# Dilated/sliding attention ahead of a squared-ReLU FFN: attention steps placed by tables, dilated values spread early, loads merged and reordered

## Chip, cores, metric

One core of one Trainium2 chip. The metric is the device time of one execution in microseconds (us); each kernel was run several times, on several chips. Of the kernel before, the record marks some as slow, being over 1.5% above its fastest. Its medians include them, the ratios leave them out.

## The reference

Attention over 8 batches, 8 heads, 576 positions, 64 values a head. Heads 0 to 3 see the last 32 positions, heads 4 to 7 see every fourth of the last 128. The result, 4608 tokens of 512 values, goes through an FFN with 2048 hidden values.

```python
def _attn_ref(q, k, v):
    scores = scale * np.matmul(q, k.transpose(0, 1, 3, 2))
    rel = pos[:, None] - pos[None, :]
    mask_plain = (rel >= 0) & (rel < 32)
    mask_dil = (rel >= 0) & (rel < 128) & (rel % 4 == 0)
    # ... where(mask, scores, -1e9), softmax over the last axis ...
    return np.matmul(attn, v)

def _moe_ref(x, w_in, w_out):
    h = np.maximum(x @ w_in, 0.0)
    return h * h @ w_out
```

## The kernel before

Heads are handled in four pairs, 0 and 1 plain, 2 and 3 dilated, in the order 0, 2, 1, 3. For each pair and batch there are seven kinds of step: transpose q, transpose k (TensorE, then copies out of PSUM by the scalar engine for plain q and by the vector engine for the rest), scores in two halves (matmuls, Exp on the scalar engine, mask multiply on the vector engine), for dilated pairs the spread of the values (two vector copies from the place where they were loaded, tile `vd`, into the block-diagonal tile `vbd`), and PV in two halves (value and sum matmuls into PSUM, Ln and Exp on the scalar engine for the reciprocal, a vector multiply into `xT`).

The FFN runs in nine tiles of 512 tokens, 32 groups of four 128x512 matmuls each: 16 of the first layer (relu on the scalar engine, square on the vector engine) and 16 of the second. A group's place is called a slot. Attention steps of batch b are emitted between the groups of tile b-1, and each engine's timeline shows its instructions in the order of emission. PV is the product of probabilities and values; PSUM is the memory in which matmul results stand until an engine copies them out.

```python
p_pool  = ...(name="p", bufs=2)                     # masked probabilities
ps_f    = ...(name="ps_f", bufs=4, PSUM)            # FFN, batch 0's scores, spare PV
ps_a    = ...(name="ps_a", bufs=2, PSUM)            # transposes, scores
ps_o, ps_d = ... bufs=1 each, PSUM                  # PV values, PV sums

def spread_v(b, e):                                 # dilated pairs only
    for hl in range(2):
        rows = slice(64 * hl, 64 * hl + 64)
        nc.vector.tensor_copy(vbd[b % 2][rows, e, 0:8, rows], vds[b][rows, e - NE // 2, :, :]...)

def attention_steps(b, base, pace, at):
    steps = []
    for x, e in enumerate(ORDER):                   # ORDER = (0, 2, 1, 3)
        s = base + pace * x
        if e >= NE // 2:
            steps.append((s + at[4], lambda e=e: spread_v(b, e)))
        steps.append((s + at[0], lambda e=e: t_main(b, e, "q")))
        steps.append((s + at[1], lambda e=e: t_main(b, e, "k")))
        steps.append((s + at[2], lambda e=e: scores(b, e, 0)))
        steps.append((s + at[3], lambda e=e: scores(b, e, 1)))
        steps.append((s + at[4], lambda e=e: pv(b, e, 0)))
        steps.append((s + at[5], lambda e=e: pv(b, e, 1)))
    return [(min(s, 2 * NF * b - 1), f) for s, f in steps]

for e in ORDER:                                     # all loads go out by GpSimd
    load_qk(0, [e])
    load_v(0, [e])
# ... w_in in two pieces, w_out in four ...
zero_halves(vbd[1], nc.gpsimd)                      # two memsets
for e in ORDER:
    load_qk(1, [e])
    load_v(1, [e])

first_attention(0)                                  # batch 0, a fixed three-stage loop
# ...
steps += attention_steps(1, 13, 6, (0, 1, 3, 4, 6, 8))
steps += attention_steps(2, G, 7, (0, 1, 4, 5, 7, 9))       # G = 32 slots
for b in range(3, B):
    steps += attention_steps(b, G * (b - 1) - 6, 8, (0, 2, 5, 6, 9, 12))
# ... emit group g, then all steps whose slot is <= g ...
```

The softmax here doesn't subtract the row's maximum and nothing guards it: scores larger than these inputs give would overflow.

## Time and profile before

| | before |
|---|---|
| median of 3 runs (all 7 of the first study rounds, 4 of them marked slow) | 384.47 us (383.85, from 378.11 to 386.62) |
| span of the profiled run | 376.8 us |
| TensorE busy | 318.7 us, 85% |
| vector, scalar, GpSimd busy | 200.4, 214.8, 90.7 us |

The page of the profiled run of the kernel before, engines (PE is TensorE's matmuls, PEld its weight loads, DVE the vector engine, ACT the scalar engine, POOL GpSimd) and four rows of its 40 slices (a digit is the busy share of a slice of 9.4 us in tenths; PEclk is TensorE's granted clock):

```profile
PE 318.7 (85%) x2389; PEld 177.7 (47%) x2432; DVE 200.4 (53%) x568; ACT 214.8 (57%) x437; POOL 90.7 (24%) x132
...
PE   1657979558789969996999699969998899999995
...
DVE  7784436445746756475647564765457552411410
...
PEclk9999989959999999999999999998999699999999
DMA  9999998294008900980098009900110002002002
```

TensorE stays at nine tenths only in the last fifth, where no attention is left. From slice 14 on it dips once in every fourth slice, which is once in each FFN tile, and deeper in slices 8 and 9, the end of tile 0. The clock row dips in some of the same places. Loads are dense in the first six slices and come in bursts after that.

### The profile page before, as it was taken

What the parts mean: (1) busy time and instruction counts of PE and PEld (TensorE: products, weight loads), DVE (VectorE), ACT (ScalarE), POOL (GpSimd) and SP (SyncE); (2) the same over time, 40 slices, a digit from 0 to 9 for tenths busy, and PEclk for the clock granted to TensorE, in tenths of its full rate; (3) what the DMA queues carried; (4) which work ended last, traced back from release to release, by engine and by line L of the source; (5) the groups of instructions that cost most, each with busy time, mean ns of one, the idle gap of its engine ahead of it and who ended that gap; (6) DMA issues with size and microseconds to landing.
All of it is one profiled execution on the core that took longest, in us unless ns stands there. A gap on an engine that the chain in (4) does not pass through costs nothing.

```text
span 376.8 us, 6323 instructions
## 1 busy us (share of the span) xinstructions
PE 318.7 (85%) x2389; PEld 177.7 (47%) x2432; DVE 200.4 (53%) x568; ACT 214.8 (57%) x437; POOL 90.7 (24%) x132
## 2 busy tenths in 40 slices
PE   1657979558789969996999699969998899999995
PEld 1534534334445535554555355535554455544542
DVE  7784436445746756475647564765457552411410
ACT  3545744537656775577656765675578444633621
POOL 8952862261007300620062007200000000000000
PEclk9999989959999999999999999998999699999999
DMA  9999998294008900980098009900110002002002
GB/s 104 150 214 208 158 139 113 57 146 42 1 30 131 143 3 7 181 114 2 4 177 121 1 3 168 133 0 2 57 56 3 0 30 84 0 30 84 0 30 84
DMA packets 51917, 28.32 MB, mean 75 GB/s; under 512 B 27696, under 2 KB 45744, under 8 KB 51888
## 3 DMA queue, kind: packets, MB, share of 16 engines
q0 software_dynamic: 46560, 18.38, 43.0%
q1 hardware_dynamic: 5184, 9.44, 6.8%
q8 instruction: 19, 0.31, 0.3%
q10 hardware_dynamic: 144, 0.11, 0.1%
q14 instruction: 10, 0.08, 0.1%
HBM read 36.81 MB, written 9.44 MB: 123 GB/s over the span
## 4 chain that ended last, share of the span: by engine, by line
PE 67%; ACT 13%; DVE 11%; issue 5%; POOL 2%; DMA 1%; ACTq 0%; DVEq 0%; POOLq 0%
PE pf L336 30%; PE pf L347 26%; ACT qT L193 5%; DVE kbd L198 4%; PE po L279 3%; PE pa L170 3%; ACT h2T L340 3%; PE pd L279 2%; DVE vbd L154 2%; ACT rec L282 2%; PE pa L230 2%; ACT rec L281 2%; DMA qb<-in_q_dram 1%; DVE xT L285 1%; DVE h2T L341 1%
## 5 line engine op out<-in xcount | busy, mean ns | idle before, releaser
L336 PE MATMUL pf<-xT,w_in_sb 128*128 128x512 bf16 x555 | 140.3, 390 | 1.9 <-DVE xT L285 0.5
L347 PE MATMUL pf<-w_out_sb,h2T 128*128 128x512 bf16 x554 | 135.9, 382 | 1.2
L340 ACT ACTIVATE h2T<-pf 128x512 bf16<-128x512 f32 x144 | 85.3, 595 | 36.3 <-PE pf L336 34.7
L341 DVE TENSOR_TENSOR h2T<-h2T 128x512 bf16<-128x512 bf16 x144 | 60.1, 424 | 69.7 <-ACT h2T L340 68.7
L336 PEld LDWEIGHTS <-w_in_sb 128*128 128x128 bf16 x576 | 60.5, 115 | 48.3 <-issue 6.0
L347 PEld LDWEIGHTS <-h2T 128*128 128x128 bf16 x576 | 51.5, 98 | 49.9 <-issue 1.1
L281 ACT ACTIVATE rec<-pd 128x288 f32<-128x288 f32 (+2 forms) x60 | 24.7, 411 | 41.5 <-PE pd L279 41.5
L353 ACT COPY osb<-pf 128x512 f32<-128x512 f32 x36 | 21.1, 585 | 42.3 <-PE pf L347 42.0
L279 PE MATMUL po<-pt,vbd 128*128 128x96 bf16 (+1 forms) x300 | 21.9, 207 | 26.0 <-DVE vbd L154 22.1
L279 PEld LDWEIGHTS <-vbd 128*128 128x128 bf16 x320 | 20.6, 104 | 41.1 <-DVE vbd L154 26.1
L236 ACT ACTIVATE pt<-pa 128x352 bf16<-128x352 f32 (+2 forms) x56 | 28.0, 501 | 18.1 <-PE pa L230 8.7
L193 ACT COPY qT<-pa 64x288 bf16<-64x288 bf16 x64 | 30.3, 474 | 11.7 <-PE pa L170 11.2
L285 DVE TENSOR_TENSOR xT<-po,rec 128x288 bf16<-128x288 f32 x30 | 13.7, 458 | 40.6 <-ACT rec L282 39.5
L116 POOL DMA_DIRECT2D qb<-in_q_dram x10 | 7.5, 746 | 104.7 <-PE pa L170 80.3
L198 DVE COPY kbd<-pa 64x288 bf16<-64x288 bf16 x64 | 30.4, 475 | 0.7
L282 ACT ACTIVATE rec<-rec 128x320 f32<-128x320 f32 (+1 forms) x64 | 28.4, 443 | 2.0
L138 POOL DMA_DIRECT2D vd<-in_v_dram x32 | 19.4, 609 | 30.0 <-DMA qb<-in_q_dram 14.4
L134 POOL DMA_DIRECT2D vbd<-in_v_dram x32 | 24.1, 762 | 4.1 <-DMA w_in_sb<-in_moe_w_in_dram 4.0
L292 DVE TENSOR_TENSOR xT<-po,rec 128x320 bf16<-128x320 f32 (+1 forms) x30 | 13.8, 460 | 20.1 <-ACT rec L282 17.1
L180 DVE COPY qT<-pa 64x288 bf16<-64x288 bf16 x64 | 19.4, 304 | 7.5 <-PE pa L170 6.8
L170 PE MATMUL pa<-mk,qb 72*128 72x72 bf16 x256 | 14.8, 205 | 8.6 <-DMA qb<-in_q_dram 8.6
L279 PE MATMUL pd<-pt,mk 128*128 128x160 bf16 (+5 forms) x150 | 21.3, 243 | 0.0
(48 smaller groups left out, 240.3 us busy)
## 6 DMA issues: line engine op xcount, KB each, us to landing
out_dram<-osb SPq DMA_DIRECT2D x36, 256.0 KB, 2.0
qb<-in_q_dram POOLq DMA_DIRECT2D x12, 288.0 KB, 6.7
kb<-in_k_dram POOLq DMA_DIRECT2D x12, 288.0 KB, 8.4
vbd<-in_v_dram POOLq DMA_DIRECT2D x32, 72.0 KB, 8.7
vd<-in_v_dram POOLq DMA_DIRECT2D x32, 64.0 KB, 4.9
w_in_sb<-in_moe_w_in_dram POOLq DMA_DIRECT2D x2, 1024.0 KB, 11.0
w_out_sb<-in_moe_w_out_dram POOLq DMA_DIRECT2D x4, 512.0 KB, 17.5
qb<-in_q_dram POOLq DMA_DIRECT2D x8, 144.0 KB, 4.9
```

The costliest lines, as they stand in the source:

```text
L134: nc.gpsimd.dma_start(dst[rows, e, :, rows], v[b, h].rearrange("(i p) d -> p i d", p=64))
L170: nc.tensor.transpose(pv_[:, hl, PT * pos : PT * pos + PT], rbs[b][nm][:, 2 * e + hl, P * jp : P * jp + P], ident[0:PT, 0:PT])
L193: nc.scalar.copy(qT[rows, e, :].rearrange("p (u a j) -> p j u a", a=JT // 2, j=2)[:, jj, :, :], src.rearrange("p (a u) -> p u a", a=JT // 2),)
L198: nc.vector.tensor_copy(kbd[rows, e, :, rows].rearrange("p i (u a j) -> p j i u a", a=JT // 2, j=2)[:, jj, :, :, :], src.rearrange("p (a i ...
L236: nc.scalar.activation(pt[:, off : off + n], ps[:, 0:n], ACT.Exp, scale=SCALE)
L279: nc.tensor.matmul(oo, lh, rh, start=(x == 0), stop=(x == len(g) - 1), skip_group_check=True)
L281: nc.scalar.activation(rec[:, 0:n], d[:, 0:n], ACT.Ln)
L282: nc.scalar.activation(rec[:, 0:n], rec[:, 0:n], ACT.Exp, scale=-1.0)
L336: nc.tensor.matmul(ps1[:, :], w_in_sb[:, kt, 512 * (f // 4) + f % 4 : 512 * (f // 4) + 512 : 4], xT[:, kt, tk0 : tk0 + NT], start=(kt == 0 ...
L340: nc.scalar.activation(h2[:, f, :], ps1[:, :], ACT.Relu)
L341: nc.vector.tensor_tensor(out=h2[:, f, :], in0=h2[:, f, :], in1=h2[:, f, :], op=ALU.mult)
L347: nc.tensor.matmul(cur[m][:, :], h2[:, f, P * m : P * m + P], w_out_sb[:, f, :], start=(f == 0), stop=(f == NF - 1),)
```

## The change

The intent: place every step of the first three batches by a table, so that no chain of waits is left bare at a tile's end; make the steady pipeline of batches 3 to 7 one slot longer between k and scores (q and k go out a slot earlier; with the base at -7 instead of -6, scores and PV keep their slots); emit the dilated spread with the q transposes instead of with PV; and bring q and k ahead of the values in larger transfers.

```diff
-    p_pool = ...(tc.tile_pool(name="p", bufs=2))
+    p_pool = ...(tc.tile_pool(name="p", bufs=4))
+FIRST = "q0 k0 q2 a0 b0 k2 k1 a2 q1 q3 v2 o0 a1 b1 k3 o1 v3 b2 p0 a3 b3 o2 p2 p1 o3 p3".split()
+EARLY = {
+    1: ("15:q0 16:k0 18:q1 19:k1 22:q2 22:a0 23:b0 24:k2 24:v2 24:a1 25:o0 26:v3 26:b1 27:q3 27:p0 27:a2 "
+        "27:o1 29:k3 29:b2 29:p1 29:o2 30:a3 30:b3 30:p2 31:o3 31:p3"),
+    2: ("0:k0 0:q0 5:a0 5:k2 6:v2 9:q2 9:v3 9:b0 12:o0 13:a2 13:b2 15:p0 15:k1 15:q1 18:k3 18:o2 18:a1 21:q3 "
+        "21:p2 23:o1 24:b1 24:a3 25:b3 25:p1 28:o3 31:p3"),
+}
-    for e in ORDER:
-        load_qk(0, [e])
-        load_v(0, [e])
+    load_qk(0, [0])
+    load_qk(0, [2, 3])
+    load_qk(0, [1])
+    load_v(0, [0, 2, 1, 3])
     ... w_in in pieces of 512, 512 and 1024 columns instead of two of 1024 ...
     zero_halves(vbd[1], nc.gpsimd)
-    for e in ORDER:
-        load_qk(1, [e])
-        load_v(1, [e])
+    load_qk(1, [0, 1, 2, 3])
+    load_v(1, [0, 1, 2, 3])
+    ... in step(): pv(b, e, "op".index(what), spare=early and what == "p")    # early is b < 2; before, batch 0 only ...
-    first_attention(0)
+    for code in FIRST:
+        step(0, code)
-    steps += attention_steps(1, 13, 6, (0, 1, 3, 4, 6, 8))
-    steps += attention_steps(2, G, 7, (0, 1, 4, 5, 7, 9))
+    ... batches 1 and 2 from EARLY: "slot:step" ...
     for b in range(3, B):
-        steps += attention_steps(b, G * (b - 1) - 6, 8, (0, 2, 5, 6, 9, 12))
+        steps += attention_steps(b, G * (b - 1) - 7, 8, (0, 2, 6, 7, 10, 13, 0))   # last: the spread
```

In the codes q and k are transposes, a and b the score halves, v the spread, o and p the PV halves; the digit is the pair.

`spare` now holds for batch 1 too. Its second PV half writes to tiles of `ps_f` instead of waiting for the single `ps_o` and `ps_d` tiles.

More of the change, by code (lines that the diff above doesn't have):

```diff
@@ L13 @@
 RES = 4
+ORDER = (0, 2, 1, 3)
+FIRST = "q0 k0 q2 a0 b0 k2 k1 a2 q1 q3 v2 o0 a1 b1 k3 o1 v3 b2 p0 a3 b3 o2 p2 p1 o3 p3".split()
+EARLY = {
+    1: (
+        "15:q0 16:k0 18:q1 19:k1 22:q2 22:a0 23:b0 24:k2 24:v2 24:a1 25:o0 26:v3 26:b1 27:q3 27:p0 27:a2 "
+        "27:o1 29:k3 29:b2 29:p1 29:o2 30:a3 30:b3 30:p2 31:o3 31:p3"
+    ),
+    2: (
+        "0:k0 0:q0 5:a0 5:k2 6:v2 9:q2 9:v3 9:b0 12:o0 13:a2 13:b2 15:p0 15:k1 15:q1 18:k3 18:o2 18:a1 21:q3 "
+        "21:p2 23:o1 24:b1 24:a3 25:b3 25:p1 28:o3 31:p3"
+    ),
+}
 def _masks() -> np.ndarray:
@@ L72 @@
     vd_pool = ctx.enter_context(tc.tile_pool(name="vd", bufs=2))
-    p_pool = ctx.enter_context(tc.tile_pool(name="p", bufs=2))
+    p_pool = ctx.enter_context(tc.tile_pool(name="p", bufs=4))
     r_pool = ctx.enter_context(tc.tile_pool(name="r", bufs=2))
@@ L294, in pv, with step @@
             )
-    ORDER = (0, 2, 1, 3)
+    def step(b: int, code: str):
+        what, e = code[0], int(code[1])
+        first, early = b == 0, b < 2
+        if what in "qk":
+            t_main(b, e, what)
+        elif what in "ab":
+            scores(b, e, "ab".index(what), *((ps_f, "pf") if first else ()))
+        elif what == "v":
+            spread_v(b, e)
+        else:
+            pv(b, e, "op".index(what), spare=early and what == "p")
     def attention_steps(b: int, base: int, pace: int, at):
-        steps = []
+        out = []
         for x, e in enumerate(ORDER):
-            s = base + pace * x
-            if e >= NE // 2:
-                steps.append((s + at[4], lambda e=e: spread_v(b, e)))
-            steps.append((s + at[0], lambda e=e: t_main(b, e, "q")))
-            steps.append((s + at[1], lambda e=e: t_main(b, e, "k")))
-            steps.append((s + at[2], lambda e=e: scores(b, e, 0)))
-            steps.append((s + at[3], lambda e=e: scores(b, e, 1)))
-            steps.append((s + at[4], lambda e=e: pv(b, e, 0)))
-            steps.append((s + at[5], lambda e=e: pv(b, e, 1)))
-        return [(min(s, 2 * NF * b - 1), f) for s, f in steps]
-    def first_attention(b: int):
-        o = ORDER
-        for x in range(NE + 2):
-            if x >= 2 and o[x - 2] >= NE // 2:
-                spread_v(b, o[x - 2])
-            for nm, half in (("q", 0), ("k", 1)):
-                if x < NE:
-                    t_main(b, o[x], nm)
-                if 1 <= x <= NE:
-                    scores(b, o[x - 1], half, ps_f, "pf")
-                if x >= 2:
-                    pv(b, o[x - 2], half, spare=half == 1)
+            for what, off in zip("qkabopv", at):
+                if what != "v" or e >= NE // 2:
+                    out.append((base + pace * x + off, b, f"{what}{e}"))
+        return out
     def ffn_groups(t: int):
@@ L375 @@
     nc.vector.tensor_copy(mask_d[:, 352:416], mk[:, 96:160])
-    for e in ORDER:
-        load_qk(0, [e])
-        load_v(0, [e])
-    for c in range(2):
+    load_qk(0, [0])
+    load_qk(0, [2, 3])
+    load_qk(0, [1])
+    load_v(0, [0, 2, 1, 3])
+    for c0, c1 in ((0, 512), (512, 1024), (1024, 2048)):
         nc.gpsimd.dma_start(
-            w_in_sb[:, :, 1024 * c : 1024 * c + 1024],
-            moe_w_in[:, 1024 * c : 1024 * c + 1024].rearrange("(kt p) f -> p kt f", p=P),
+            w_in_sb[:, :, c0:c1], moe_w_in[:, c0:c1].rearrange("(kt p) f -> p kt f", p=P)
         )
@@ L400 @@
         groups += ffn_groups(t)
-    steps += attention_steps(1, 13, 6, (0, 1, 3, 4, 6, 8))
-    steps += attention_steps(2, G, 7, (0, 1, 4, 5, 7, 9))
+    for b, table in EARLY.items():
+        for x in table.split():
+            slot, code = x.split(":")
+            steps.append((G * (b - 1) + int(slot), b, code))
     for b in range(3, B):
-        steps += attention_steps(b, G * (b - 1) - 6, 8, (0, 2, 5, 6, 9, 12))
+        steps += attention_steps(b, G * (b - 1) - 7, 8, (0, 2, 6, 7, 10, 13, 0))
     steps.sort(key=lambda x: x[0])
@@ L407 @@
         t = g // G
-        if g % G == 0:
-            if t + 2 < B:
-                load_qk(t + 2, [0, 1, 2, 3])
-                load_v(t + 2, [0, 1, 2, 3])
+        if g % G == 0 and t + 2 < B:
+            load_qk(t + 2, [0, 1, 2, 3])
+            load_v(t + 2, [0, 1, 2, 3])
         group()
         while steps and steps[0][0] <= g:
-            steps.pop(0)[1]()
+            step(*steps.pop(0)[1:])
 _INS = ['q', 'k', 'v', 'moe_w_in', 'moe_w_out']
```

## The prediction

> **What bounds it.** I cut the run into stages first, by one table of engine time per stretch. Columns: stretch, its length, then busy time and (in brackets) instruction count of the matmul engine, weight loads, vector, scalar and GpSimd engine, then granted clock, DMA share, GB/s.
>
> ```profile
> 0.00:31.50 31.50, 13.64 (x159) 11.21 (x160) 23.34 (x58) 13.92 (x30) 24.12 (x35) 1.00 1.09 162
> 31.50:82.20 50.70, 38.83 (x286) 21.39 (x291) 24.31 (x69) 26.17 (x55) 25.71 (x37) 0.89 0.99 131
> 82.20:124.50 42.30, 36.68 (x302) 20.18 (x307) 25.29 (x73) 27.66 (x58) 9.62 (x14) 0.97 0.60 61
> 124.50:317.40 192.90, 174.42 (x1398) 98.18 (x1424) 113.36 (x336) 122.62 (x255) 31.27 (x46) 0.97 0.38 60
> 317.40:376.80 59.40, 55.11 (x252) 26.76 (x254) 14.07 (x33) 24.42 (x42) 0.00 (x0) 1.00 0.11 40
> ```
>
> They are: attention of batch 0 alone; FFN tile 0 with batch 1 beside it; tile 1 with batch 2; tiles 2 to 6 with batches 3 to 7; tiles 7 and 8 and the last store, with no attention left. TensorE is the bound from 31.5 us on, and its queue runs in program order, so its idle time is what can be won: 11.9 us in tile 0, 5.6 in tile 1, 18.5 in tiles 2 to 6 (3.7 a tile). The last stage is almost full (27.7 us a tile). Where a steady tile loses it, the matmul engine's timeline says; the brackets hold the idle time before a row and its releaser:
>
> ```profile
> 162.26 0.39 PE L230 MATMUL pa<-qT,kbd 128*128 128x96 bf16 x5 [0.49 <-DVE kbd L198]
> ...
> 174.01 1.03 PE L336 MATMUL pf<-xT,w_in_sb 128*128 128x512 bf16 x4
> 178.01 0.35 PE L279 MATMUL po<-pt,vbd 128*128 128x96 bf16 x5 [2.98 <-DVE vbd L154]
> ```
>
> The same two waits return in every steady tile (2.98 to 3.19 and 0.47 to 0.49). The copy waited for, the spread of the dilated values, is cheap; the vector engine was held up before it:
>
> ```profile
> 174.57 0.43 DVE L341 TENSOR_TENSOR h2T<-h2T 128x512 bf16<-128x512 bf16 x1 [0.44 <-ACT h2T L340]
> 177.01 0.42 DVE L341 TENSOR_TENSOR h2T<-h2T 128x512 bf16<-128x512 bf16 x1 [2.02 <-ACT h2T L340]
> 177.36 0.60 DVE L154 COPY vbd<-vd 64x512 bf16<-64x512 bf16 x2
> ```
>
> The square at 177.01 waits for a relu, and the scalar engine was copying the next q for 1.92 us from 174.44. Relu, square, spread and PV matmul stand in four queues behind that copy; the spread's data had been there for long.
>
> Tile 0 loses most at its end, where batch 1's last steps were all clamped to the last slot (a slot is one FFN group of four matmuls, 0.865 us) and run as a bare latency chain:
>
> ```profile
> 72.22 0.34 PE L279 MATMUL po<-pt,vbd 128*128 128x32 bf16 x5 [1.65 <-DVE xT L292]
> ...
> 77.09 0.26 PE L215 MATMUL pa<-qT,kbd 128*128 128x96 bf16 x1 [3.85 <-DVE kbd L184]
> ...
> 81.19 0.48 PE L279 MATMUL po<-pt,vbd 128*128 128x96 bf16 x5 [1.46 <-DVE xT L285]
> ```
>
> **The Trainium skill.** "TensorE: Matmul & The Clock Gate", Part 1, says that about a 3.4 us idle window drops the TensorE clock to half, until about as long a busy one. The trace agrees at gaps near that length: after the 3.19 us gap before 253.83, eight FFN matmuls took 3.28 us, where elsewhere eight take 1.89. Of five equal gaps only two were followed by this, as a free-running window would have it. The same page ("Architectural detail") calls the scalar and vector engines strict FIFO; the hold-up above is that. "SBUF — State Buffer", "Who interferes with whom", says a 2-port vector copy and a GpSimd instruction lock each other out for a whole instruction. It agrees: the spread's median is 291 ns, but one took 2074 ns beside the GpSimd memset of 17.9 to 22.0 us. "DMA: Bandwidth & Descriptors", "Bandwidth", favours larger transfers. Here a 144 KB q load lands in 4.9 us and a 288 KB one in 6.7, but in the first 30 us the queues share a rate of 104 to 214 GB/s that is already saturated, so I give merging little.
>
> **The change, part by part.** No arithmetic is added or removed; the compiled TensorE queue has 4866 rows before and after.
>
> *Steady tiles.* Spread moves from the slot of its PV step to ten slots earlier, with the q transposes. That removes the 2.98 us. Scores move from three slots after the k transposes to four (0.865 us more slack, against a wait of 0.49), which removes that too. A tile without both: 37.9 - 2.98 - 0.49 = 34.4. A check from below: 128 FFN matmuls at 0.216 are 27.7; attention adds, from start-to-start times, 8 transpose groups at 0.26, 8 PV halves at 0.36 and 1.5 for scores, together 6.5: 34.2. The extra scalar slack is real but not large: the scalar engine is busy 15.07 us in the first-layer half of a tile (20.2 us now, 17.2 then), 88%. I take 34.5. Five tiles: 172.5 against 192.9. Of the 20.4, some 3.5 are the two half-clock stretches after the gaps (these tiles' halves are 21.9 and 23.1 where the others are 20.2).
>
> *Tile 1.* Batch 2's table spreads its steps over slots 0 to 31 instead of bunching them. The early waits (1.29, 1.67, 1.40, 0.49 and the slow matmuls at 82 to 85.5) should mostly go; but two scores come three slots after their transposes behind a busy vector queue, and the last PV half is in slot 31, so the next tile waits for Ln, Exp and multiply (0.43 + 0.44 + 0.46, with latencies 1.5). 34.5 + 2.5 = 37.0 against 42.3.
>
> *Tile 0.* Batch 1 starts two slots later, in slot 15, and spreads its last PV steps over slots 25 to 31; k to score is now six slots, not two, for the first head pair (a 2.32 us wait). In the last five slots I count 7.7 us of TensorE work (5 groups at 0.865, 4 scores, 6 PV halves, 2 transpose groups) and 9.2 us of scalar work (4 exp at 0.5, seven Ln/Exp pairs at 0.87, two output copies). So it is scalar-bound there, and then the chain of the last half remains: 3 to 4 us of idle at the end, and 1 us of slow clock after it. 34.5 + 4 + 1 = 39.5 against 50.7. Loads do not stop it: the moved bytes up to slot 15 are as before and in the old run all weights were in by about 36 us, the q and k of batch 1 would follow by about 43 (estimate: 1.18 MB at the 176 GB/s of that stretch), and slot 15 comes at about 41 (28 + 15 x 0.865), slot 22 at 48.
>
> *Start.* q and k of all pairs now come ahead of the values, which are written in small pieces, and the steps interleave so that a wait of one pair is filled by another. The first two loads are in the same place, so the first transposes stay at 5.07 us. Then the vector queue bounds: two k copies of 1.93, two dilated q of 1.26, two dilated k of 1.76, eight masks 2.9, eight output multiplies 3.7, spreads 0.6 and 3.0 (the memset is still near), in sum 20.1 us from 6.8, plus 1 us waiting for q of pair 2: about 28 us, and 0.5 for the last chain. The old one finished its last multiply at 33.3. I take 4.5 us off: 31.5 becomes 27.0. The first third of w_in arrives in 512 columns, so weights do not take over: about 2.3 MB at 140 GB/s is 16 to 18 us.
>
> *Rest.* Tiles 7 and 8 are untouched: 59.4. Sum: 27.0 + 39.5 + 37.0 + 172.5 + 59.4 = 335.4, against 376.8. The measured time is 1.75 above the span (378.55), so 337.2. The unprofiled runs of before are slower than the profiled one (384.47 against 378.55); I read that as more of the five gaps falling into the slow clock, 1.7 us each, and fewer such gaps are left after. I add 1: 338.
>
> **The rivals.** *The wait moves to the scalar engine.* At 88% in the first-layer halves, relus may fall behind by more than the four PSUM buffers of the FFN. For it: the 1.92 us q copies. Against it: four buffers are 3.4 us of run-ahead, and the old stall came from the spread, not from an FFN matmul waiting. It would return 1 to 2 us a tile: 343 to 348. *Loads bound the first 70 us.* DMA is at about full share until 60 us; with FFN starting earlier and batch 1 in four large loads, a value load could land after slot 24, and the in-order vector queue would hang behind its spread. For it: the loads of batch 1 end near 49 us, the first spread of batch 1 comes at about 50. It would eat 3 to 6 us of tile 0: 341 to 344. *Only the spread counts*: the tables gain nothing on tiles 0 and 1 because scalar work is the same and bunched at their ends. Then 384.47 less 20 and 4.5, about 360; against it, the old chains from 70 to 82 us had both engines idle most of the time. *Better than thought*: start at 24, tile 0 at 37, tile 1 at 35 give 328 to 330.
>
> **Range and chances.** The steady saving alone is 5% and its cause is seen in each tile; losing it all and the rest as well is needed for no gain. The range is the sum of the rivals' sizes: 329 to 350. Faster by over 2% 0.97, within 2% 0.02, slower 0.01.
>
> **What would show it.** The spread should vanish as a releaser of PV matmuls from tile 2 on; steady tiles should take 34 to 35 us at clock 1.00; FFN should start at 26 to 29 us; tile 0 should end with one gap of 3 to 4 us, and its length be about 40. Wrong would be: FFN matmuls waiting for relu buffers, first transposes or spreads of batch 1 waiting for loads, or a steady tile above 36.

## The result

| | before | after |
|---|---|---|
| median | 384.67 us (4 runs) | 338.07 us (4 runs, 337.76 to 338.37) |
| ratio, 95% interval | | 0.8796 (0.8733 to 0.8859) |
| span of the profiled run | 376.8 us | 336.3 us |
| TensorE busy, idle | 318.7, 58.1 us | 309.4, 26.9 us |

A ratio is the mean time of one kernel's fast runs over that of the other's of the same rounds, so not quite the ratio of the medians quoted beside it. The page of the changed kernel, the same rows (a slice is 8.4 us here):

```profile
PE 309.4 (92%) x2432; PEld 175.7 (52%) x2432; DVE 200.4 (60%) x568; ACT 211.5 (63%) x437; POOL 87.3 (26%) x127
...
PE   1438999989999999999999999999999999999995
...
DVE  7797457969755784587549664966486724303400
...
PEclk9999999999999999999999999999999999999999
```

Vector work is the same 200.4 us to the digit. TensorE is at nine tenths from the fifth slice to the last but one, but for one eight, and the clock dips are gone. The same table by stages as in the prediction, the stages cut at the same events (first FFN matmul; start of tiles 1, 2 and 7):

```profile
0.00:31.00 31.00, 13.27 (x161) 11.03 (x161) 25.06 (x57) 12.93 (x29) 22.92 (x33) 1.00 1.06 150
31.00:67.20 36.20, 34.88 (x291) 20.04 (x289) 23.91 (x69) 25.60 (x54) 18.55 (x28) 1.00 1.27 161
67.20:103.40 36.20, 34.95 (x311) 20.45 (x309) 25.54 (x73) 26.82 (x58) 14.53 (x21) 1.00 0.83 107
103.40:276.70 173.30, 170.63 (x1424) 97.25 (x1421) 111.86 (x336) 121.48 (x258) 31.27 (x46) 1.00 0.42 67
276.70:336.30 59.60, 55.62 (x258) 26.92 (x255) 14.06 (x33) 24.70 (x42) 0.00 (x0) 1.00 0.11 40
```

| stage | before | predicted | after |
|---|---|---|---|
| batch 0 alone | 31.5 | 27.0 | 31.0 |
| tile 0 | 50.7 | 39.5 | 36.2 |
| tile 1 | 42.3 | 37.0 | 36.2 |
| tiles 2 to 6 | 192.9 | 172.5 | 173.3 |
| tiles 7, 8, last store | 59.4 | 59.4 | 59.6 |
| span | 376.8 | 335.4 | 336.3 |

The total is right to 1 us, but two terms are wrong by 3 to 4 us each and cancel. First what went as said: the stretch of a steady tile that answers to the 2.98 us gap before 178.01 us (matmul engine's timeline of the changed kernel, no bracket where there is no idle time), and the wait of the first scores:

```profile
116.71 0.34 PE L294 MATMUL po<-pt,vbd 128*128 128x96 bf16 x5
116.89 0.33 PE L294 MATMUL pd<-pt,mk 128*128 128x192 bf16 x3
...
121.69 0.39 PE L245 MATMUL pa<-qT,kbd 128*128 128x96 bf16 x5 [0.38 <-DVE kbd L213]
```

The PV matmul of the dilated pair has no wait any more; the scores still wait 0.38 instead of 0.49 us, which I had said would go. The end of tile 0, where four bare waits had stood:

```profile
66.37 0.34 PE L294 MATMUL po<-pt,vbd 128*128 128x96 bf16 x5
...
67.20 0.81 PE L343 MATMUL pf<-xT,w_in_sb 128*128 128x512 bf16 x3
69.26 0.38 PE L343 MATMUL pf<-xT,w_in_sb 128*128 128x512 bf16 x1 [1.25 <-DVE xT L300]
```

One wait of 1.25 us is left. Three matmuls of the next tile's first group run before it, because only the fourth reads the last pair's rows of `xT`. Of the four old waits, those of 1.65 and 1.46 us were second PV halves waiting for the multiply that frees the single PV tile; here the second halves write to `pf`. e7 below, which has the old table but keeps `spare`, has neither wait, so these two went with `spare` and not with the table; what they were worth in time was not measured.

Now what went wrong. The vector engine's timeline of the changed kernel at the start, then GpSimd's, then the matmul engine's:

```profile
18.84 5.35 DVE L169 COPY vbd<-vd 64x512 bf16<-64x512 bf16 x2
```

```profile
19.79 2.14 POOL L371 MEMSET vbd<- 64x2304 bf16 x1
21.97 2.07 POOL L372 MEMSET vbd<- 64x2304 bf16 x1
```

```profile
25.17 0.53 PE L294 MATMUL po<-pt,vbd 128*128 128x96 bf16 x5 [5.74 <-DVE pt L252]
...
33.24 13.33 PE L343 MATMUL pf<-xT,w_in_sb 128*128 128x512 bf16 x61 [0.99 <-DVE xT L300]
```

The two copies of the first spread, 0.6 us elsewhere, took 5.35 us and ended with the second memset. In the kernel before they took 3.01 (0.90 and 2.07), since they began beside the last 0.8 us of the first memset (vector engine's timeline of the kernel before, then GpSimd's):

```profile
19.17 3.01 DVE L154 COPY vbd<-vd 64x512 bf16<-64x512 bf16 x2
```

```profile
17.88 2.06 POOL L364 MEMSET vbd<- 64x2304 bf16 x1
19.97 2.07 POOL L365 MEMSET vbd<- 64x2304 bf16 x1
```

In the changed kernel TensorE waited 5.74 us for a mask multiply that stood behind the two copies, and the long run of FFN matmuls began at 33.24 us, where before it had begun at 33.34. So against the kernel before the start gained nothing.

### The profile page after: what moved, and what is told of

Read it like the earlier page. It is cut to its first block, busy times and chain, and to the rows that moved or that the text cites. A ratio compares the mean times of both kernels' runs of the same rounds, so it can differ in the third digit from the quotient of the medians.

```text
span 336.3 us, 6386 instructions
## 1 busy us (share of the span) xinstructions
PE 309.4 (92%) x2432; PEld 175.7 (52%) x2432; DVE 200.4 (60%) x568; ACT 211.5 (63%) x437; POOL 87.3 (26%) x127
## 4 chain that ended last, share of the span: by engine, by line
PE 78%; ACT 8%; DVE 8%; issue 3%; DMA 2%; POOL 0%; ACTq 0%; POOLq 0%
PE pf L354 37%; PE pf L343 29%; PE pa L185 4%; DVE kbd L213 3%; ACT h2T L347 3%; PE po L294 2%; DMA qb<-in_q_dram 2%; PE pd L294 2%; ACT qT L208 2%; PE pa L245 2%; DVE vbd L169 2%; ACT rec L296 1%; ACT rec L297 1%; PE pa L230 1%; PE pa L231 1%
## 5 line engine op out<-in xcount | busy, mean ns | idle before, releaser
L343 PE MATMUL pf<-xT,w_in_sb 128*128 128x512 bf16 x576 | 134.8, 379 | 3.3 <-DVE xT L300 3.0
L347 ACT ACTIVATE h2T<-pf 128x512 bf16<-128x512 f32 x144 | 83.9, 595 | 25.6 <-PE pf L343 24.0
L348 DVE TENSOR_TENSOR h2T<-h2T 128x512 bf16<-128x512 bf16 x144 | 58.5, 423 | 54.1 <-ACT h2T L347 53.1
L296 ACT ACTIVATE rec<-pd 128x288 f32<-128x288 f32 (+2 forms) x56 | 23.1, 412 | 30.8 <-PE pd L294 30.8
L300 DVE TENSOR_TENSOR xT<-po,rec 128x288 bf16<-128x288 f32 x28 | 12.8, 458 | 28.3 <-ACT rec L297 27.9
L297 ACT ACTIVATE rec<-rec 128x288 f32<-128x288 f32 (+2 forms) x64 | 28.4, 443 | 2.0
L294 PE MATMUL po<-pt,vbd 128*128 128x96 bf16 (+1 forms) x280 | 19.9, 203 | 6.0 <-DVE pt L252 5.7
L185 PEld LDWEIGHTS <-qb 72*128 72x128 bf16 x256 | 12.8, 102 | 15.9 <-DMA qb<-in_q_dram 8.7
L307 DVE TENSOR_TENSOR xT<-po,rec 128x320 bf16<-128x320 f32 (+1 forms) x28 | 13.0, 463 | 13.1 <-ACT rec L297 12.5
## 6 DMA issues: line engine op xcount, KB each, us to landing
w_in_sb<-in_moe_w_in_dram POOLq DMA_DIRECT2D x1, 1024.0 KB, 11.6
```

What stands on the lines that cost most here:

```text
L185: nc.tensor.transpose(pv_[:, hl, PT * pos : PT * pos + PT], rbs[b][nm][:, 2 * e + hl, P * jp : P * jp + P], ident[0:PT, 0:PT])
L294: nc.tensor.matmul(oo, lh, rh, start=(x == 0), stop=(x == len(g) - 1), skip_group_check=True)
L296: nc.scalar.activation(rec[:, 0:n], d[:, 0:n], ACT.Ln)
L297: nc.scalar.activation(rec[:, 0:n], rec[:, 0:n], ACT.Exp, scale=-1.0)
L343: nc.tensor.matmul(ps1[:, :], w_in_sb[:, kt, 512 * (f // 4) + f % 4 : 512 * (f // 4) + 512 : 4], xT[:, kt, tk0 : tk0 + NT], start=(kt == 0 ...
L347: nc.scalar.activation(h2[:, f, :], ps1[:, :], ACT.Relu)
```

## The experiments

Each is the changed kernel with one edit, unless said otherwise. Twelve kernels, all correct (there is no e2 or e5). The medians of the kernel before in their rounds were 383.85 to 384.56 us, so medians of different rounds can be set beside each other to about a microsecond. Against the kernel before, the record's verdict is "faster" for eight of the twelve and "unclear" for e1, e3, e4 and e6, in whose rounds only three of its runs were fast; the readings below compare with the changed kernel.

### What held the start

**e1.** Theory: a port lock between vector copy and GpSimd memset. Rival: the values, loaded last now, had not landed.

```diff
-    zero_halves(vbd[1], nc.gpsimd)
     for code in FIRST:
         step(0, code)
+    zero_halves(vbd[1], nc.vector)
```

> Changed kernel, but the zeroing of batch 1's value tile moves from GpSimd (two memsets of 2.1 us at 19.8 to 24.0 us) to the vector engine after batch 0's attention. Theory (port lock): the first spread pair, 5.35 us from 18.84 us, only waited for the two GpSimd memsets; it should take about 0.6 us, the 5.74 us wait of the PV matmul before 25.17 us should fall to about 1 us, the long run of FFN matmuls should start at about 28.5 us instead of 33.24, and the time should be 333 to 334.5 us. Rival (late data): the dilated values, loaded last now, had not landed; then the spread still ends near 24 us and the time stays at 338.

Measured: 336.34 us (335.49 to 337.33), clock 0.997 in the profiled run. The vector engine's and the matmul engine's timelines of e1:

```profile
19.23 0.70 DVE L169 COPY vbd<-vd 64x512 bf16<-64x512 bf16 x2
...
28.48 0.46 DVE L300 TENSOR_TENSOR xT<-pf,rec 128x288 bf16<-128x288 f32 x1 [0.32 <-ACT rec L297]
```

```profile
26.73 0.38 PE L343 MATMUL pf<-xT,w_in_sb 128*128 128x512 bf16 x1
30.08 13.76 PE L343 MATMUL pf<-xT,w_in_sb 128*128 128x512 bf16 x63 [2.98 <-DMA w_in_sb<-in_moe_w_in_dram]
```

The spread falls to 0.70 us: the data were there and the memsets were the cause. The last multiply of batch 0 ends 4.25 us earlier (28.94 against 33.19). Yet the time falls by 1.7 us only, since FFN now waits 2.98 us for weights and its long run begins 3.16 us earlier: the expected number was missed because a new wait, of the kind that I had ruled out, took the place. (The profiled run is 2.7 us shorter; the other three ran at clocks of 0.989 to 0.994, and what the rest went to was not looked into.) The waits in the compiled program explain it: the first weight load waits for the first piece of `w_in` alone; the second, for all three pieces, though it reads columns of the first one only. The trace agrees: the first FFN matmul runs at 26.73 us, the second at 30.08, just after the last piece landed at 29.94. All pieces were one tile, and the dependences were drawn too wide; e9 tests it. So cutting `w_in` into three in the change does not let the FFN start earlier.

**e9.** As e1, with the three pieces in tiles of their own.

```diff
-    w_in_sb = const.tile([P, KT, DFF], bf16, name="w_in_sb")
+    w_in_sb = [const.tile([P, KT, 512 * n], bf16, name=f"w_in{i}") for i, n in enumerate((1, 1, 2))]
```

> As e1 (late zeroing on the vector engine), and the three column pieces of w_in lie in three tiles of their own instead of in one. In e1 the second weight load of the FFN waited for all three transfers (2.98 us, until the last landed at 29.94 us). Theory: with separate tiles the first FFN matmuls wait for the first piece alone, which landed by about 23 us; that gap goes, the long run starts at about 27 instead of 30.08 us, and the time is about 3 us below e1: 332 to 334. Rival: with the weights still arriving, the third piece holds up group 8 at about 34 us (it landed at 29.94, so it should not), or batch 1's loads hold up slot 15; then 335 to 336.

Measured: 334.17 us (333.36 to 334.77), just above the range expected. Matmul timeline of e9:

```profile
28.09 13.33 PE L343 MATMUL pf<-xT,w_in 128*128 128x512 bf16 x61 [0.98 <-DVE xT L300]
...
43.95 0.43 PE L185 MATMUL pa<-mk,kb 72*128 72x72 bf16 x8 [1.00 <-DMA kb<-in_k_dram]
```

The weight wait is gone and the long run begins at 28.09 us. A third wait shows up: the transposes of batch 1 in slots 15 and 16 wait 0.23 and 1.00 us for their q and k, which stand behind `w_out` in the queue. So of the 5.15 us that FFN starts earlier, 3.9 arrive in the time.

**e6, e10, e11: is the new start worth anything?** e6 has the old order of batch 0's steps and loads; e10 has it with the two hindrances removed as in e9; e11 is e9 with the old step order only.

```diff
-FIRST = "q0 k0 q2 a0 b0 k2 k1 a2 q1 q3 v2 o0 a1 b1 k3 o1 v3 b2 p0 a3 b3 o2 p2 p1 o3 p3".split()
+FIRST = "q0 k0 q2 a0 k2 b0 q1 a2 o0 k1 b2 p0 v2 q3 a1 o2 k3 b1 p2 a3 o1 b3 p1 v3 o3 p3".split()   # e6, e10, e11
-    load_qk(0, [0]) ... load_v(0, [0, 2, 1, 3])
+    for e in ORDER: load_qk(0, [e]); load_v(0, [e])                                               # e6, e10
```

> Changed kernel with the old order of batch 0's steps and the old order and sizes of its twelve q, k and value loads, all else kept (also the split of w_in and batch 1's merged loads). Theory: the new start won nothing as it stands, because its spread met both GpSimd memsets where the old one met only one; time 337 to 339.5. Rival: the new order is worth its 4.5 us and is hidden by something else; then about 342.

Measured: 340.26 us (339.54 to 340.81), between the theory's range and the rival's 342. Here too the spread met both memsets, and took 4.35 us, where I had expected it to meet one, as in the kernel before (there it was the end of the first and the whole second). So the new start is worth about 2.2 us even as it stands.

> As e9, but with the old order of batch 0's steps and the old order and sizes of its loads. Theory: with both hindrances gone the new order shows its worth: its last vector multiply comes at 28.9 us, the old order's about 3 us later (33.6 less 2 to 3 of memset wait), so this runs 2.5 to 4 us longer than e9, about 336. Rival: the new order is worth nothing even then: equal to e9 within 1 us.

Measured: 336.54 us (336.30 to 337.23), 2.4 us above e9: just under the range expected, well above the rival.

> As e9, but batch 0's steps in the old order; its loads stay in the new order and sizes. e9 was 334.17 us, e10 (old steps and old loads) 336.54. Theory: the gain of about 2.4 us lies in the order of the steps, and the new loads by themselves only delay what the old order wants early (values of the first pair, q of the second), so this is no better than e10: 336.5 to 339. Rival: the load order carries the gain, then 334 to 335.

Measured: 336.95 us (336.62 to 337.68), as e10 within 0.4. The new load order alone is worth nothing with the old steps; the gain of the start lies in the order of the steps, or in the two together. The new steps with the old loads were not run.

### The steady pipeline

**e3.** The spread of batches 3 to 7 goes back to the slot of its PV step; all else is kept.

```diff
-steps += attention_steps(b, G * (b - 1) - 7, 8, (0, 2, 6, 7, 10, 13, 0))    # q k a b o p v
+steps += attention_steps(b, G * (b - 1) - 7, 8, (10, 0, 2, 6, 7, 10, 13))   # v q k a b o p
```

> Changed kernel with the dilated spread of batches 3 to 7 put back into the slot of its first PV step, all else kept. Theory: each of the five steady tiles gets its gap of about 3 us before a PV matmul back, with the spread as releaser, 338 + 15 = 353 us, and up to 358 where gaps are followed by half clock. Rival: the longer pipeline (scores a slot later, PV a slot later, four probability tiles) had removed the gap by itself; then 338 to 341.

Measured: 354.17 us (351.95 to 357.08). Matmul timeline of e3, two of its five tiles:

```profile
156.21 0.50 PE L294 MATMUL po<-pt,vbd 128*128 128x96 bf16 x5 [2.62 <-DVE vbd L169]
...
157.32 3.67 PE L343 MATMUL pf<-xT,w_in_sb 128*128 128x512 bf16 x12
```

```profile
194.48 0.35 PE L294 MATMUL po<-pt,vbd 128*128 128x96 bf16 x5 [2.62 <-DVE vbd L169]
...
195.11 2.76 PE L343 MATMUL pf<-xT,w_in_sb 128*128 128x512 bf16 x12
```

The gap returns in each steady tile (five waits, 13.1 us), and the longer pipeline does not remove it. The same gap of 2.62 us is followed once by twelve matmuls in 3.67 us and once by twelve in 2.76: whether a gap costs slow clock as well differs from tile to tile, and the runs do not show why. That is also why the runs scatter: in e3's four runs the time goes from 351.95 us at a mean clock of 0.990 to 357.08 at 0.975, and in the kernel before, in the fast runs of e12's rounds, from 380.72 at 0.963 to 385.80 at 0.947. (Not every low clock costs time: a run of e6 at 0.973 took 340.17 us, among 339.54 to 340.81 for its others at 1.000.) The profiled run of the changed kernel has no wait above 1.25 us after the start; its four runs have a clock of 0.998 to 1.000 and a scatter of 0.6 us.

**e4.** The kernel before, with only the spread of batches 3 to 7 moved to the slot of the q transposes.

```diff
-    steps.append((s + at[4], lambda e=e: spread_v(b, e)))
+    steps.append((s + (at[4] if early is None else early), lambda e=e: spread_v(b, e)))   # early=0 for b >= 3
```

> Kernel before with one edit: the dilated spread of batches 3 to 7 is emitted in the slot of the q transposes. Theory: the five 3 us gaps go and with them the slow-clock stretches after them, so 384.5 - 15 - 4 = about 365 us (362 to 368); the 0.5 us waits of the first scores stay. Rival: in the old pacing another wait takes the gap's place (scalar engine behind), then above 375.

Measured: 366.95 us (366.67 to 368.26). As forecast in size, but not for the reason in full. Matmul timeline of e4, a steady tile:

```profile
143.45 0.39 PE L230 MATMUL pa<-qT,kbd 128*128 128x96 bf16 x5 [0.92 <-DVE kbd L198]
...
161.14 0.39 PE L230 MATMUL pa<-qT,kbd 128*128 128x96 bf16 x5 [0.48 <-DVE kbd L198]
```

The 2.98 us gap is gone, but a wait of 0.92 us of the second plain pair's scores, absent before, has taken part of its place. A tile takes 36.4 us (from 124.95 to 161.37), against 37.9 before and 34.65 after the change. So the early spread alone gives 1.5 us a tile beside the slow clock that it saves, and the longer pipeline about the other 1.8 (a comparison of two kernels that also differ in the number of probability tiles): each covers a wait that the other leaves.

**e12.** Could the remaining 0.38 us be had by moving the k transposes one slot forward? On top of e9:

```diff
-(0, 2, 6, 7, 10, 13, 0)
+(0, 1, 6, 7, 10, 13, 0)
```

> As e9, with the k transposes of batches 3 to 7 one slot earlier, so that a pair's k copies no longer stand behind the output multiply of the pair before in the vector queue. Theory: the remaining 0.38 to 0.40 us wait of the first scores in each steady tile goes, five times 0.4 = 2 us: 332 to 332.7. Rival: the copies then meet the relu squares and the wait moves elsewhere: 334 as in e9.

Measured: 345.48 us (344.77 to 346.10), 11.3 us worse than e9. Matmul timeline of e12:

```profile
109.10 0.34 PE L294 MATMUL po<-pt,vbd 128*128 128x32 bf16 x5 [1.06 <-DVE xT L307]
...
119.03 0.33 PE L294 MATMUL po<-pt,vbd 128*128 128x96 bf16 x5 [1.27 <-DVE xT L300]
```

The wait of the scores went, as expected. But the k copies (2.0 us) now stand ahead of the output multiply in the vector queue, and that multiply frees the single PSUM tile of PV, which the second half needs three slots later. Two new waits of 1.06 and 1.27 us in five tiles are 11.6 us. Neither theory nor rival had thought of this.

### The tables of batches 1 and 2

Besides the lines shown, both edits emit the spread of batches 3 to 7 just before the q transposes of its slot instead of just after; a steady tile still takes 34.65 us (in e8 from 129.10 to 163.75). Both keep `spare` for batch 1.

```diff
+steps += [(min(s, 31), *r) for s, *r in attention_steps(1, 13, 6, (6, 0, 1, 3, 4, 6, 8))]   # e7, instead of EARLY[1]
+steps += [(min(s, 63), *r) for s, *r in attention_steps(2, G, 7, (7, 0, 1, 4, 5, 7, 9))]    # e8, instead of EARLY[2]
```

> Changed kernel with batch 1's steps by the old formula (start in slot 13, late ones clamped to the last slot). Theory: the bare chain at the end of tile 0 and the early 2.3 us wait return, and with them slow clock; tile 0 goes from 36.2 to 48 to 50 us, time 350 to 353. Rival: the old clamping hurt only because of something else that the change removed (load order, two probability tiles); then under 344.

Measured: 348.23 us (347.79 to 348.84), clock 0.989 to 0.990: 10.2 us for the table of batch 1, a little under the range expected and far above the rival. Of the old waits come back 2.38 us before the first scores and most of the bare chain at the end of the tile, though not the 1.65 and 1.46 us for the single PV tile, since `spare` is kept (matmul timeline of e7):

```profile
73.96 0.26 PE L230 MATMUL pa<-qT,kbd 128*128 128x96 bf16 x1 [4.55 <-DVE kbd L199]
```

> Changed kernel with batch 2's steps by the old formula. Theory: tile 1 was 42.3 us before, of which about 2 us was slow clock left over from tile 0's end; without that it goes from 36.2 to about 40, time 341 to 343, with waits of the first scores of 1.3 to 1.4 us and of one PV of 1.7 us back. Rival: tile 1 was only slow because of tile 0, then 338 to 339.

Measured: 346.86 us (345.88 to 348.12), 8.8 us for the table of batch 2, nearly twice what I expected. The waits told of came (1.53 and 1.45 us of scores, 1.67 of a PV), and one that I had left out: the second dilated pair's PV, in slot 28 of the tile, waits 2.12 us for its spread, which the old formula puts in the same slot. So part of this table's worth is the early spread again.

### The fastest version

e13 adds three things to e9: the earlier k of e12; batch 1's plain q and k loaded ahead of the second half of `w_out`; batch 2's last PV step in slot 30 instead of 31. e14 is e13 without the earlier k.

```diff
     for c in range(4):
+        if c == 2:
+            load_qk(1, [0, 1])
         nc.gpsimd.dma_start(w_out_sb[...], ...)
-    load_qk(1, [0, 1, 2, 3])
+    load_qk(1, [2, 3])
-        "... 28:o3 31:p3"
+        "... 28:o3 30:p3"
```

> As e12, and batch 1's q and k of the plain heads are loaded ahead of the second half of w_out (in e9 their transposes waited 0.23 and 1.00 us for them), and batch 2's last PV step is in slot 30 instead of 31 (0.73 us wait at the start of tile 2). Theory: these three waits of 2 us go as well: 330.5 to 331.5. Rival: w_out then lands too late for slot 18 or 19 and the wait only changes its name: 332 to 333.

Measured: 343.10 us (342.30 to 343.27): far from 331, since e12's waits are in it; against e12 it is 2.4 us faster.

> As e13 without the earlier k transposes, which e12 showed to cost 11 us (two waits of 1.06 and 1.27 us a tile for the single PSUM output tile). Theory: the parts are independent, so e9 (334.17) less what e13 won over e12 (345.48 - 343.10 = 2.4) gives 331 to 332.5, the fastest of the study. Rival: what e13 won was slack beside its own waits, then 333.5 to 334.5.

Measured: 332.52 us (331.97 to 333.25), ratio to the kernel before 0.8678 (0.8636 to 0.8719), clock 1.00. The fastest, 5.5 us under the changed kernel by the medians and a hair above the range expected. The waits of batch 1's transposes for their loads and the 0.73 us at the start of tile 2 are gone from its list of waits.

### The sum

Put back one at a time, the parts cost: the spread of batches 3 to 7 16.1 us (e3), batch 1's table 10.2 (e7), batch 2's table 8.8 (e8), the start 2.2 (e6). Together 37.3 of the 46.6 us. The longer steady pipeline was not put back alone with the early spread in place; e4 against the changed kernel gives an estimate for it, 36.4 less 34.65 us in five tiles, or 8.8 (the whole stage, 181.4 against 173.3 us, gives 8.1). That closes the sum to about 1 us, which is no proof: the parts are not independent, as e3 and e4 show, and no part of it was worked out for `spare`. Not tried alone: `spare` for batch 1; the four probability tiles, which the new start needs, since it has three pairs open at once, and the merging of batch 1's loads.

## Why the prediction was right, and where not

- **Steady tiles: right, 172.5 against 173.3.** The main half of the mechanism holds: the spread was held up in its queue (e3 brings the gap back, e4 removes it). Wrong was that the second wait would go: 0.38 of 0.49 us stayed. It is not slack between k and scores that is missing; the k copies stand behind the previous pair's output multiply in the vector queue, and e12 shows that putting them ahead costs 11.3 us with the one PV tile.
- **Slow clock: right.** I added 1 us to the profiled time for it, and it was not needed (profiled 338.17, median 338.07). That before's scatter goes with slow clock is now seen run by run.
- **Tile 0: the bare chain went as said, the bound at the tile's end was wrong**, 39.5 against 36.2. The failed step is "it is scalar-bound there": 9.2 us of scalar work against 7.7 of TensorE. In the last slots, 58.6 to 67.2 us, TensorE was busy for 8.58 of 8.60 us, the scalar engine for 7.23, and only 1.45 of scalar work were left after it. My TensorE sum was too small (it counts six PV halves where the table has seven), the scalar sum counted durations where instructions overlap at their edges, and I forgot that three matmuls of the next group run before the last pair is needed. 1.25 us of wait came of it instead of 3 to 4, and no slow clock after it.
- **Tile 1: right, a little low in gain**, 37.0 against 36.2: its last PV half cost 0.74 us, not 1.5, for the same reason.
- **Start: wrong**, 27.0 against 31.0. The failed step is the term "spreads 0.6 and 3.0 (the memset is still near)": the pair took 5.35 us, because it now met nearly the whole of both memsets. I had seen the lock in the trace and mis-sized it, when the quoted rule said that the loser waits for whole instructions. That is 2.35 us of the miss. The rest is idle time of the vector engine between 6.8 and 33.2 us: 2.17 and 0.35 us for q transposes where I had put 1, and five waits of 0.26 to 0.36 us in the last chain where I had put 0.5 in all. With these the vector queue ended at 33.19 us, not at about 28.4. "Weights do not take over" was the second error in that part, hidden in the changed kernel and laid open by e1: the first piece, a quarter of `w_in` and not a third, was to come at 16 to 18 us, but its load was only issued at 15.5, and the three took 5.5 to 11.6 us to land.
- **The rivals.** Scalar engine behind: did not come. Loads: they did not bound the changed kernel's tile 0, but they are the next bound as soon as the start is mended (e1, e9). Only the spread counts, about 360 us (outside the range of 329 to 350 that was to cover the rivals): refuted by e7 and e8.

The total within 0.1 us of the median is luck: +4.0 at the start against -3.3 and -0.8 in tiles 0 and 1.

## What to carry to other kernels

With in-order queues, look not only at how long the awaited instruction takes but at what stands ahead of it in its queue; the cure is to emit it where its queue is free, and cheap work whose data are there can go ten slots ahead. Moving one instruction forward puts it ahead of others: before doing so, ask which buffer those others free; in e12 the k copies went ahead of the multiply that frees the single PV tile. When a start is mended, the next wait is close behind; follow it from wait to wait (memset, weights, loads), and check that pieces of a load really are waited for piece by piece.

## What the Trainium skill lacked or had wrong

- "SBUF — State Buffer", "Who interferes with whom", has the lock, and that the loser waits for a whole instruction. It could say what a series does: a pair of 0.3 us copies lost 4.75 us to two memsets of 2.1 us in a row (3.24 and 2.08 us for the two copies, one after the other). That whoever issues first gets the port does not come out here: the first copy is recorded as starting 0.95 us before the first memset, while GpSimd was issuing weight loads, and yet ended 0.15 us after it. Issuing alone need not hold such a pair: in e1 it took 0.70 us wholly beside the issue of the weight loads (18.25 to 20.55 us). What held the first copy before the memset's recorded start stays open; starts on GpSimd are rough in the profile.
- "TensorE: Matmul & The Clock Gate", Part 1, names an idle window of about 3.4 us. Gaps of 2.62 us, as the profile brackets them, were enough in some of the tiles of e3 (3.67 us for twelve matmuls against 2.76 after an equal gap), so that a shorter gap can cost clock too; in the kernel before, the recorded mean clock and the time of a run went together (0.963 and 380.72 us, 0.947 and 385.80 us).
- No page has it: transfers into column pieces of one tile were waited for together by the second weight load, so that the second FFN matmul waited until the last piece landed (2.98 us in e1, none with a tile for each piece in e9).
